# A spectral layer with other factors, and head and tail stages that share pools, in a forward-and-backward kernel on one Trainium2 core

## The chip, the cores and the metric

The kernel runs on one core of a Trainium2 chip (trn2). Times are device microseconds (us) of one execution, given as the median of several. A profile is one execution; its span is a little shorter than the time. A program on one core gave no slow run. TensorE, VectorE, ScalarE, GpSimd and SyncE are called PE, DVE, ACT, POOL and SP in the lines of the profile, and PEld is TensorE's weight load. An engine that starts DMAs holds a queue for them: SPq is the one of SyncE.

## The reference

One residual block, its output, and the gradients of all its inputs for a given output gradient. Everything is bfloat16 outside; S = 2048 positions, D = 576 channels, F = 4608 hidden channels.

```python
mod = (silu(c) @ w_mod).reshape(1, 6, 1, -1)            # sa, ca, ga, sb, cb, gb
h  = layernorm(x) * (1 + ca) + sa
x1 = x + ga * irfft2(rfft2(h) * (w_r + 1j * w_i))       # spectral layer over (S, D)
h2 = layernorm(x1) * (1 + cb) + sb
out = x1 + gb * (((h2 @ w_gate) * (h2 @ w_up)) @ w_down)
# returned: out, and d/d(x, w_r, w_i, w_gate, w_up, w_down, c, w_mod) of sum(out * grad_out)
```

## The kernel before

Three parts run one after another. The **head** computes the modulation, the first LayerNorm, the spectral layer forward, and the "gradient groups": the output gradient times the transposed `w_down`, stored to memory (`ghhT_d`) for later. The **main loop** has 18 iterations over the hidden channels: gate and up projections, their gradients and the three weight gradients. The change leaves its code alone. The **tail** computes the second LayerNorm's backward, the down-projection, the spectral layer backward, the first LayerNorm's backward, and the gradients of the modulation.

The spectral layer is a 2-D transform as matrix products. Before the change it went channel transform, 128-point transform, then, after a transpose on TensorE of 73 blocks, a 16-point transform whose output is scattered by strided evictions (an eviction, `evac` in the code, copies a result of TensorE out of PSUM, the memory that matmuls write to):

```python
def chainF(hT, T, ring, sm, fps, name):
    Vp = ring.tile([128, NG, 128], BF, name=name + "Vp", tag="r")     # NG = 73
    for t in range(NT):                                               # NT = 16
        for cc in range(2):
            for m in range(5):
                nc.tensor.matmul(zp[:, :FP], lhsT=hT[:, t, m, :], rhs=T["RD"][:, m, cc, :], ...)
            evac(zt[:, cc, :], zp[:, :FP])
        # ... [cut: 128-point transform into vp, strided eviction into Vp] ...
    dma_T(VT, Vp, fps)                     # transposes on TensorE, through PSUM
    for g0 in range(0, NG, 4):
        # ... [cut: 16-point transform, two strided evictions for each group of 4] ...
```

The gradient groups transpose `w_down` on TensorE.

```python
for j in range(FB4):
    for m in range(4):
        nc.tensor.transpose(ptw[:, m, :], wdn[:, j, m * 128:(m + 1) * 128], ident[:])
    # ... [cut: fifth block, evictions to wdT and wdL] ...
for j in range(0, FB4, 2):
    for sp in range(2):
        for k in range(2):
            for i in range(2):             # 64 rows: wdL, block 4
                nc.tensor.matmul(pts[k][i][:], lhsT=wdL[r, j // 2, :], rhs=goT[r, tss[k], 4, :], start=True, stop=False)
        for k in range(2):
            for i in range(2):
                for m in range(4):         # 128 rows
                    nc.tensor.matmul(pts[k][i][:], lhsT=wdT[:, m, ...], rhs=goT[:, tss[k], m, :], start=False, stop=(m == 3))
```

Each stage has its own pools, so a stage starts when the one before has given its memory back; tables are loaded as fp32 and cast; sums over rows go through GpSimd accumulators and a round trip through memory (`dm_d`).

## Time and profile before

| | before |
|---|---|
| time, median of 4 | 2083.85 us (2070.23 to 2090.29) |
| span of the profile | 2068.4 us |
| head, to the main loop's first 128-row matmul | 479 us |
| main loop, to its last matmul | 1007 us |
| tail | 582 us |

The boundaries in the table are starts and ends of single matmuls in the trace.

These are lines of the page of the kernel before. The first gives, for each engine, its busy time, share of the span and number of instructions. The others cut the span in 40 slices; a digit is the busy share of a slice in tenths, and PEclk is the granted clock of TensorE in tenths.

```profile
PE 1617.6 (78%) x11711; PEld 1058.5 (51%) x11711; DVE 1027.7 (50%) x2082; ACT 533.0 (26%) x1059; POOL 324.8 (16%) x329
...
PE   2086988399999999999999999999757982626321
...
DVE  1567776035443334444444444333486333388974
...
PEclk8587999699999999999999999999868995867555
```

The middle, slices 9 to 28, is a plain stretch of 9: TensorE is the bound there. On both sides TensorE falls to between 0 and 8 tenths in most slices, and its clock in many of them. The average of 78% hides that the two ends have another limit than the middle.

The table of stretches of the kernel before says where. Its columns are: stretch, its length, busy time (and instructions) of each engine, granted clock, DMA share, GB/s.

```profile
core 0: us, PE busy (x) PEld busy (x) DVE busy (x) ACT busy (x) POOL busy (x), PEclk, DMA share, GB/s
0.00:103.00 103.00, 14.80 (x71) 5.93 (x71) 39.23 (x90) 18.75 (x26) 20.35 (x25) 0.65 0.80 246
...
362.00:380.00 18.00, 0.00 (x0) 0.00 (x0) 0.07 (x1) 0.00 (x0) 0.00 (x0) 0.52 1.13 223
...
478.00:1486.00 1008.00, 1004.09 (x7776) 708.07 (x7776) 422.54 (x1008) 257.63 (x522) 93.19 (x134) 1.00 0.68 129
...
1887.00:2011.00 124.00, 43.48 (x182) 16.25 (x180) 106.68 (x123) 34.31 (x62) 86.52 (x49) 0.55 0.24 74
2011.00:2068.00 57.00, 6.66 (x16) 3.78 (x16) 21.57 (x16) 17.25 (x9) 0.00 (x0) 0.56 0.41 156
```

TensorE does 14.8 us of work in the first 103 us. From 362 to 380 no engine works at all. In the main loop it is busy 1004 of 1008 us. In the last 181 us it is busy 50 us, with the clock at half.

What holds everything at 362 is one instruction on SyncE's queue. Its line in the queue's timeline of the kernel before gives start, length, engine, source line and operands:

```profile
352.24 24.25 SPq L466 DMA_TRANSPOSE h2T<-h2p  x1
```

The stores of the gradients stand behind it on that queue (the next is issued at 376.6 us), and TensorE waits 20.0 us for the buffers that they hold.

And this is one group of DVE in the first LayerNorm's backward, of the kernel before: count, busy time in us, mean ns of one.

```profile
L737 DVE SCALAR_TENSOR_TENSOR t<-gn,n1b 128x576 bf16<-128x576 bf16 x16 | 22.9, 1430 | 0.6
```

### The profile page before, as it was taken

The page shows a single profiled execution, that of the slowest core. Times are in us where ns is not written, and L with a number is a line of the kernel's source. Part 1 is how long each engine was busy: PE and PEld are TensorE (multiplying, and loading weights), DVE is VectorE, ACT ScalarE, POOL GpSimd, SP SyncE. Part 2 cuts the span into 40 slices and gives each one's busy share as a digit, 9 for nine tenths or more (in the row PEclk, how much of TensorE's full clock was granted, in tenths as well). Part 3 has the DMA queues.
Part 4 walks back from the last instruction along what each step waited for, and adds up shares of the span by engine and source line. Part 5 has one row for each costly group of instructions (what it writes and reads, how often), then busy time and mean ns, then how long its engine had stood idle before and what let it go on. Part 6 is the DMA issues. An engine that isn't in the chain of part 4 may idle for free. (4 is left out here: it accounts for less than half of the span.)

```text
span 2068.4 us, 29648 instructions
## 1 busy us (share of the span) xinstructions
PE 1617.6 (78%) x11711; PEld 1058.5 (51%) x11711; DVE 1027.7 (50%) x2082; ACT 533.0 (26%) x1059; POOL 324.8 (16%) x329
## 2 busy tenths in 40 slices
PE   2086988399999999999999999999757982626321
PEld 0054533145666677777666666666635762423100
DVE  1567776035443334444444444333486333388974
ACT  1254533022222222222222222222110001234133
POOL 1200001001111001011111111100102335224740
PEclk8587999699999999999999999999868995867555
DMA  7834365537766666666677776675576633071223
GB/s 274 218 121 170 134 240 131 134 114 158 136 108 134 125 130 125 130 136 136 143 132 136 140 123 138 120 129 109 147 268 256 237 122 133 31 284 45 84 99 126
DMA packets 387660, 302.78 MB, mean 146 GB/s; under 512 B 305697, under 2 KB 352929, under 8 KB 382785
## 3 DMA queue, kind: packets, MB, share of 16 engines
q1 hardware_dynamic: 363808, 203.55, 39.8%
q0 software_dynamic: 23712, 97.34, 17.2%
q8 instruction: 91, 1.49, 0.3%
q14 instruction: 49, 0.39, 0.1%
HBM read 138.63 MB, written 89.71 MB: 110 GB/s over the span
## 5 line engine op out<-in xcount | busy, mean ns | idle before, releaser
L536 DVE TENSOR_TENSOR guT<-ghh,gT 128x512 bf16<-128x512 bf16 x144 | 61.2, 425 | 480.3 <-DMA out_dram<-wl 384.0
L553 PE MATMUL abp<-wT,guT 128*128 128x288 bf16 x1152 | 283.0, 286 | 0.0
L552 PE MATMUL abp<-wT,ggT 128*128 128x288 bf16 x1152 | 283.0, 286 | 0.0
L530 PE MATMUL abp<-h2T,wgu 128*128 128x512 bf16 x1152 | 261.1, 380 | 0.0
L558 DVE TENSOR_TENSOR acc<-acc,abp 128x288 f32<-128x288 f32 x544 | 240.7, 453 | 20.5 <-PE abp L553 5.3
L574 PEld LDWEIGHTS <-h2p 128*128 128x128 bf16 x2304 | 225.3, 98 | 26.7
L530 PEld LDWEIGHTS <-wgu 128*128 128x128 bf16 x1152 | 106.8, 98 | 149.5 <-issue 30.5
L542 POOL DMA_DIRECT2D hhT_d<-hhT x36 | 33.2, 923 | 911.4 <-DVE hhT L534 773.6
L648 PE MATMUL u3p<-wdr,hl 128*128 128x288 bf16 x1152 | 150.8, 294 | 23.0 <-DMA hl<-hhT_d 12.7
L426 PE MATMUL u4p<-goT,wdT 128*128 128x512 bf16 x576 | 161.6, 410 | 0.0
L566 PE MATMUL gwp<-gon,hh_sf 128*128 128x288 bf16 x1152 | 144.8, 286 | 3.0 <-DMA hh_sf<-hhT 3.0
L648 PEld LDWEIGHTS <-hl 128*128 128x128 bf16 x1152 | 115.4, 100 | 56.1 <-DMA hl<-hhT_d 13.2
L567 ACT CAST so<-gwp 128x288 bf16<-128x288 f32 x72 | 28.7, 398 | 394.3 <-PE gwp L566 394.3
L566 PEld LDWEIGHTS <-hh_sf 128*128 128x128 bf16 x1152 | 112.3, 98 | 32.5 <-DMA hh_sf<-hhT 4.3
L574 PE MATMUL gwp<-gg_sf,h2p 128*128 128x256 bf16 x1152 | 128.7, 273 | 0.0
L574 PE MATMUL gwp<-gu_sf,h2p 128*128 128x256 bf16 x1152 | 128.7, 273 | 0.0
L553 PEld LDWEIGHTS <-guT 128*128 128x128 bf16 x1152 | 112.6, 98 | 30.3
L552 PEld LDWEIGHTS <-ggT 128*128 128x128 bf16 x1152 | 112.7, 98 | 30.0
L311 PE MATMUL yp<-T_IR,ut 128*128 128x288 bf16 (+1 forms) x384 | 75.8, 334 | 55.9 <-ACT gh L731 55.9
L532 ACT CAST gT<-abp 128x512 bf16<-128x512 f32 x144 | 84.3, 585 | 85.4 <-PE abp L530 85.4
L575 ACT CAST wo<-gwp 128x256 bf16<-128x256 f32 x144 | 53.6, 372 | 197.5 <-PE gwp L574 196.1
L137 DVE CAST ghh_st<-u4p 128x512 bf16<-128x512 f32 x72 | 49.1, 688 | 110.8 <-PE u4p L426 59.9
(380 smaller groups left out, 2113.0 us busy)
## 6 DMA issues: line engine op xcount, KB each, us to landing
ghhT_d<-ghh_st SPq DMA_DIRECT2D x36, 512.0 KB, 3.2
ghh<-ghhT_d POOLq DMA_DIRECT2D x36, 512.0 KB, 9.5
hhT_d<-hhT POOLq DMA_DIRECT2D x36, 512.0 KB, 6.8
hl<-hhT_d SPq DMA_DIRECT2D x8, 2304.0 KB, 9.7
out_dram<-wo SPq DMA_DIRECT2D x36, 256.0 KB, 2.3
gxc<-gx_d SPq DMA_DIRECT2D x8, 1152.0 KB, 8.8
wm<-in_w_mod_dram SPq DMA_DIRECT2D x2, 3456.0 KB, 14.2
wdn<-in_B_w_down_dram SPq DMA_DIRECT2D x9, 576.0 KB, 6.7
```

What stands on the lines that cost most here:

```text
L311: nc.tensor.matmul(yp[:, 0:288], lhsT=ut[0:Kf, fc, cc * 128:(cc + 1) * 128], rhs=T["IR"][0:Kf, fc, cc, h * 288:(h + 1) * 288], start=(k == ...
L426: nc.tensor.matmul(pts[k][i][:], lhsT=wdT[:, m, (j + i) * 128:(j + i + 1) * 128], rhs=goT[:, tss[k], m, :], start=False, stop=(m == 3))
L530: nc.tensor.matmul(pts[k][i][:], lhsT=wgu[:, 4 * i + m, cs], rhs=h2T[:, ts_, m, :], start=False, stop=(m == 3))
L532: nc.scalar.copy(dst[:], pts[k][i][:])
L536: nc.vector.tensor_tensor(out=guT[:, ts_, :], in0=ghh[:, ts_, :], in1=gu[0][:], op=MUL)
L552: nc.tensor.matmul(pu[:, 0:288], lhsT=ggTs[j][:, t, :], rhs=wT[:, 0, j, hs_], start=(j == 0), stop=False)
L553: nc.tensor.matmul(pu[:, 0:288], lhsT=guTs[j][:, t, :], rhs=wT[:, 1, j, hs_], start=False, stop=(j == G - 1))
L558: nc.vector.tensor_tensor(out=dst, in0=dst, in1=pu[:, 0:288], op=ADD)
L566: nc.tensor.matmul(pw[:, 0:288], lhsT=hh_sf[:, j, t, :], rhs=gon[:, t, h * 288:(h + 1) * 288], start=(t == 0), stop=(t == NT - 1))
L574: nc.tensor.matmul(pw[:], lhsT=h2p[:, t, m * 128:(m + 1) * 128], rhs=sf[:, :, t, :], start=(t == 0), stop=(t == NT - 1))
L575: nc.scalar.copy(wo[:, m, :], pw[:].rearrange("q j f -> q (j f)"))
L648: nc.tensor.matmul(p2[h][:, 0:288], lhsT=hl[:, fb, ti * 128:(ti + 1) * 128], rhs=wdr[:, fb, h * 288:(h + 1) * 288], start=(fb == 0), stop= ...
```

## The change

It leaves the main loop alone and rewrites head and tail. The spectral layer does the 16-point step first (on rows that need no transpose), folds the channels into even and odd halves, and treats frequencies k and 16-k as a pair, so that each of 8 pairs is a short chain of matmul, eviction, matmul. Tables and intermediates are bfloat16. The transposed `w_down` comes by transposing DMA. GpSimd does no arithmetic; column sums are matmuls with a matrix of ones. And head and tail each have one set of pools for all their stages, so that the gradient groups (head) and the down-projection (tail) can fill TensorE while the chain of small operations runs elsewhere. Outside the main loop the order of each engine's instructions is fixed when the kernel is compiled; an engine then runs them in that order. The diff is 1454 lines; this is its core.

```diff
-def chainF(hT, T, ring, sm, fps, name): ...          # and to_group, chainI, make_hT, dma_T
+def fold(wk, h, t0, hT, T, fps, eng):                  # even/odd halves, then the 16-point step
+    nc.vector.tensor_tensor(out=eo[:, :, 0:256], in0=h[:, :, 0:256], in1=h[:, :, 576:320:-1], op=ADD)
+    # ... [cut: three more] ...
+    nc.tensor.matmul(ps[:, m, :, j, :], lhsT=eo[:, j, m * 128:(m + 1) * 128], rhs=T["BD"][:], start=True, stop=True)
+def pair_fwd(i, wk, gt, T, hT, fps, ev):               # one frequency pair forward
+    for kk, kap in enumerate((k2a, k2b)):
+        pz = fps.tile([128, 2, 512], FP32, name="pz", tag="fa")      # two PSUM slots in all
+        # ... [cut: 6 matmuls] ...
+        evac(zt[:, kk, :, :], pz[:, :, 0:FQ], ev[kk])
+    for kk in range(2):
+        px = fps.tile([128, 2, 512], FP32, name="px", tag="fa")
+        # ... [cut: 4 to 8 matmuls] ...
+        evac(X[:, kk, :, :], px[:, :, 0:FQ], ev[2 + kk])
+    return X
@@ gradient groups
-                nc.tensor.transpose(ptw[:, m, :], wdn[:, j, m * 128:(m + 1) * 128], ident[:])
+                nc.sync.dma_start_transpose(out=wdT[:, 0:4, :], in_=B_w_down[rows, 0:512])
+                nc.sync.dma_start_transpose(out=wdT[:, 4:5, :], in_=B_w_down[rows, 448:576])
+                for k in range(2):
+                    for b in range(2):
+                        for m in range(5):
+                            r = slice(0, 128) if m < 4 else slice(64, 128)
+                            nc.tensor.matmul(pg[:, b, :], lhsT=wdT[r, m, :], rhs=goT[r, ts_, m, :], start=(m == 0), stop=(m == 4))
@@ end of the head: the activations of the main loop, transposed in two pieces
-            nc.sync.dma_start_transpose(out=h2T[:]..., in_=h2p[:]...)
+                if t0 % 8 == 6:
+                    t8 = slice(t0 - 6, t0 + 2)
+                    nc.sync.dma_start_transpose(out=h2T[:, t8, :, :]..., in_=h2p[:, t8, :]...)
+                grad_group(NFB - 8 + t0 // 2, True)
@@ tail
+    for i in range(8):
+        Gy = pair_fwd(i, wk, gt, T, hT, fps, "aaaa")
+        Y = cmul(wk, Gy, load_wp(wk, i), True)
+        pair_inv(i, Y, gbt, ut, fps, "va")
+        # ... [cut: gradients of w_r and w_i] ...
+    # ... [cut: inverse transform and first LayerNorm's backward] ...
+    hl = slot(0, [128, NFB, 256], "hl")                  # down-projection, in the same pools
```

## The prediction

> **What bounds the kernel now.** The profiled span is 2068 us: head to 479, main loop to 1486, tail to the end (starts of single instructions). The table of stretches shows TensorE busy 892 of 895 us (535 to 1430) at clock 1.00: the main loop is bound by TensorE, and the change leaves its code alone. In head and tail no engine is the bound. TensorE is mostly idle for 95 us (fp32 tables are loaded and cast; `c` lands after 15 us behind a 3.4 MB load) and for 18 us at 362 (the transposing DMA of `h2p` holds the SP queue 24 us and the `ghh_st` stores wait). In the tail, stages run one after another: second-LayerNorm backward, down-projection (129 us, DVE busy 51), spectral backward at clock 0.5 to 0.8, first-LayerNorm backward (124 us, DVE busy 107; L737 takes 1430 ns beside GpSimd, the like L610 817), then 57 us of `dm_d` round trip and modulation gradients.
>
> **What the change does.** (1) Spectral transforms are refactored (16-point step first, even/odd folding, conjugate pairs); TensorE transposes and many strided evictions go. Counted matmul columns: head 552k against 563k, tail 553k against 561k. [...] (512-column matmuls start 216 ns apart). Estimated floor: 230 us each. (2) Transposed `w_down` comes by DMA. (3) bf16 tables, intermediates and modulation vectors. [...] 512 bf16 elements 425 ns, 576 fp32 750 ns. (4) GpSimd arithmetic and `dm_d`/`modb_d` round trips go; column sums move to TensorE. (5) Stages share pools, so gradient groups (head) and down-projection (tail) can fill TensorE while the chain runs on DVE and ACT.
>
> **Costs (estimates from traced durations).** Head: first gradient matmul near 30 us instead of 105; 218 us of TensorE work at 88% density; DVE 145, ACT 170 us beside it; last transposes: 300 us (before 479). Main loop: 1005 (1007). Tail: DVE 67 second LayerNorm, 63 pairs, 50 first LayerNorm, 44 modulation gradients, 18 down-projection: 242 us, of which 20 can start before the last weight gradients end. DVE and TensorE both near 230 us; with dependences 275 (582). All saving is on the critical path: the three parts are serial.
>
> **Prediction.** 300 + 1005 + 275, plus 10 for dispatch and last stores: **1590 us**, 8 in 10 between **1525 and 1680**. Faster by over 2%: 0.98; within: 0.01; slower: 0.01.
>
> **What would show each step.** First main-loop matmul at 275 to 330 us, then 1005 us unchanged. Head: TensorE at 8 to 9 tenths from 35 us. Tail 245 to 320 us: DVE 8 to 9 tenths, down-projection matmuls scattered between fold and pair matmuls, clock near 1.0. bf16 tensor_tensor of 1152 elements near 760 ns; GpSimd nearly idle.
>
> **What would make it wrong.** The scheduled order may put the down-projection last (tail +100 us). The single `hl` and output PSUM buffers could stall it. Two PSUM slots per chain could make pairs latency-bound (over 12 us each). [...] 72 small transposing DMAs may hold the SP queue and starve the gradient groups. Memory placement or DMA may slow the main loop.

The floor of 230 us for each end stands as an estimate: at the 216 ns for 512 columns that the trace of the kernel before shows, counts of 552k and 553k columns give 233 us. The 760 ns expected for 1152 bfloat16 elements lie on the line through two points of the same trace, 425 ns for a product of 512 elements and 2.57 us for one of 4624.

## More of the kernel before

A contraction of 576 is four blocks of 128 and one of 64. Note the order in which it is written: four 64-row matmuls first, then sixteen 128-row ones. The compiled order is another: the trace has 175 direct changes between its 64-row and its 128-row gradient matmuls, with only 144 of the former.

## The result, and the profile after

| | before | after |
|---|---|---|
| median, all runs of this pair | 2079.12 us (2070.23 to 2093.53, 16 runs) | 1717.72 us (1698.22 to 1723.57, 11 runs) |
| span of the profile | 2068.4 us | 1715.9 us |
| ratio | | 0.823, 95% interval 0.820 to 0.826 |

A ratio is the mean time of one kernel's runs over that of the other's of the same rounds, so it is not quite the ratio of the medians. The kernel takes 18% less time. It is 128 us slower than the predicted 1590 us, and 38 us above the top of the range.

The same lines of the page, for the kernel after:

```profile
PE 1560.4 (91%) x11196; PEld 1018.3 (59%) x11196; DVE 764.3 (45%) x1743; ACT 513.7 (30%) x881; POOL 202.8 (12%) x365
...
PE   3899999458999999999999999999999959998983
...
DVE  4733005332542355234533454235423767678831
...
PEclk9899999779999999999999999999999979999997
```

TensorE now stands at 8 and 9 almost everywhere. What is left are four notches: the first slice, slices 8 and 9 (300 to 386 us, the end of the head), slice 33 (1373 to 1416, the start of the tail), and the end.

The table of stretches of the kernel after, columns as before:

```profile
core 0: us, PE busy (x) PEld busy (x) DVE busy (x) ACT busy (x) POOL busy (x), PEclk, DMA share, GB/s
0.00:48.00 48.00, 17.75 (x71) 7.50 (x72) 20.66 (x61) 7.93 (x13) 7.82 (x19) 0.91 1.09 272
...
338.00:371.00 33.00, 8.06 (x29) 2.64 (x28) 9.46 (x22) 7.55 (x12) 8.42 (x14) 0.64 0.88 168
371.00:1385.00 1014.00, 1002.75 (x7753) 707.34 (x7752) 439.99 (x1054) 258.95 (x523) 99.84 (x148) 1.00 0.69 136
1385.00:1414.00 29.00, 13.20 (x117) 6.84 (x113) 16.97 (x38) 8.55 (x13) 8.82 (x20) 0.65 0.98 349
1414.00:1550.00 136.00, 129.70 (x1023) 94.36 (x1021) 98.85 (x169) 44.57 (x69) 24.03 (x54) 1.00 0.63 187
...
1690.00:1716.00 26.00, 2.43 (x8) 1.06 (x6) 6.08 (x15) 4.29 (x6) 1.62 (x3) 0.53 0.15 45
```

The first 48 us and the 29 us at 1385 have a DMA share near 1 (1.09 and 0.98): DMA engines, not TensorE, are full there. In the last 26 us every engine is idle for most of the time.

What TensorE waited for around the head's end, in the view of waits of the kernel after from 290 to 375 us (who waited, for what, us in total, times, longest):

```profile
PE ghp L377 <- DMA wdTh<-in_B_w_down_dram: 19.5, 1, 19.5
PE abp L480 <- DMA wgu<-in_B_w_gate_dram: 13.6, 1, 13.6
PE abp L480 <- DMA wgu<-in_B_w_up_dram: 9.8, 1, 9.8
```

Why the first of these came late is seen on SyncE's queue, of the kernel after:

```profile
295.47 10.85 SPq L418 DMA_TRANSPOSE h2T<-h2p  x1
306.49 1.84 SPq L368 DMA_TRANSPOSE wdTh<-in_B_w_down_dram  x1
308.39 1.22 SPq L369 DMA_TRANSPOSE wdTh<-in_B_w_down_dram  x1
309.78 6.84 SPq L368 DMA_TRANSPOSE wdTh<-in_B_w_down_dram  x1
```

The 24.25 us transpose of the kernel before is now two of about 11 us. The first still stands in front of the small transposes of `w_down`, and TensorE stands still for 19.5 us, which is the gap at 300 to 320 us.

And the line that answers to L737 of before:

```profile
L671 DVE SCALAR_TENSOR_TENSOR t<-gn,n1b 128x576 bf16<-128x576 bf16 x16 | 12.1, 754 | 0.3
```

The same operation on the same shapes takes 754 ns in the mean where it took 1430. But the mean misleads: in the kernel before, ten of the 16 took 757 or 758 ns, with GpSimd adding beside each of them (as far as the trace's rough times for GpSimd tell); six took 1825 to 4192. So arithmetic on GpSimd at the same time was not enough to slow it, and what set the six apart was not tested.

Set against the sum of the prediction, measured from the trace:

| part | predicted | after | difference |
|---|---|---|---|
| head, until the 17th 128-row matmul of the main loop | 300 | 371 | +71 |
| from there to the main loop's last matmul | 1005 | 1014 | +9 |
| from there to the end of the span | 275 | 331 | +56 |
| time less span (the prediction's 10 were for dispatch and last stores) | 10 | 2 | -8 |
| sum | 1590 | 1718 | +128 |

(The 17th is taken because after the first 16 the loop waits once more, 1.5 us, for its transposed activations; below, "the main loop flows" means this matmul. The first 128-row matmul, from which the 479 us of before are counted, starts at 363.6 us; by that boundary the head misses by 64 us and the loop by 17. In the kernel before, the 17th starts at 483.5 us.) The experiments have to explain 71 us of head and 56 us of tail.

### The profile page after: what moved, and what is told of

Same layout as the page of the kernel before. It is cut to its first block, busy times and chain, and to the rows that moved or that the text cites. A ratio compares the mean times of both kernels' runs of the same rounds, so it can differ in the third digit from the quotient of the medians.

```text
span 1715.9 us, 28314 instructions
## 1 busy us (share of the span) xinstructions
PE 1560.4 (91%) x11196; PEld 1018.3 (59%) x11196; DVE 764.3 (45%) x1743; ACT 513.7 (30%) x881; POOL 202.8 (12%) x365
## 4 chain that ended last, share of the span: by engine, by line
PE 82%; DMA 9%; DVE 3%; ACT 2%; issue 1%; SPq 1%; POOL 0%; DVEq 0%; ACTq 0%; POOLq 0%
PE abp L486 15%; PE gwp L530 14%; PE ghp L377 10%; PE abp L508 8%; PE abp L509 8%; PE gwp L522 7%; PE po L700 7%; PE pb L240 2%; PE abp L480 2%; PE gwp L537 2%; PE px L221 2%; DMA hh_sf<-hhT 2%; PE pv L269 1%; PE pz L206 1%; PE cs L556 1%; DMA h2T<-h2p 1%
## 5 line engine op out<-in xcount | busy, mean ns | idle before, releaser
L492 DVE TENSOR_TENSOR guT<-ghh,gT 128x512 bf16<-128x512 bf16 x144 | 61.2, 425 | 504.5 <-DMA out_dram<-wl 383.5
L700 PE MATMUL po<-wdr,hl 128*128 128x288 bf16 x1152 | 162.5, 291 | 21.8 <-DMA hl<-hhT_d 12.7
L377 PE MATMUL ghp<-goT,wdT 128*128 128x512 bf16 (+1 forms) x560 | 151.9, 386 | 3.4 <-DVE mods L325 2.3
L700 PEld LDWEIGHTS <-hl 128*128 128x128 bf16 x1152 | 111.4, 99 | 62.6 <-issue 21.4
L377 PEld LDWEIGHTS <-wdT 128*128 128x128 bf16 (+1 forms) x560 | 46.7, 97 | 97.4 <-issue 74.0
L488 ACT CAST uT<-abp 128x512 bf16<-128x512 f32 x144 | 84.3, 585 | 47.6 <-PE abp L486 45.8
```

The costliest lines, as they stand in the source:

```text
L377: nc.tensor.matmul(pg[:, b, :], lhsT=wdT[r, m, :], rhs=goT[r, ts_, m, :], start=(m == 0), stop=(m == 4))
L488: nc.scalar.copy(dst[:], pts[k][i][:])
L492: nc.vector.tensor_tensor(out=guT[:, ts_, :], in0=ghh[:, ts_, :], in1=gu[0][:], op=MUL)
L700: nc.tensor.matmul(po[:, h, 0:288], lhsT=hl[:, fb, j * 128:(j + 1) * 128], rhs=wdr[fb // 18][:, fb % 18, h * 288:(h + 1) * 288], start=(fb ...
```

## The experiments

Eighteen kernels ran, all with 3 or 5 timed rounds. The differences "from after" below are (ratio - 0.8232) x 2079 us. Each ratio has an interval of about +-6 us, so a difference from after of less than 8 us is not resolved by the times. Any edit also makes the compiler order other instructions differently, so an effect in one stage is read from that stage in the trace. That has a limit too: in runs that leave the tail's code alone (e1, e2, e3, e10, e18) the tail takes 322.1 to 330.9 us, and in runs that leave the head's alone (e4 to e9, e11) the main loop flows at 366.1 to 376.2 us. A single trace with a tail up to 9 us shorter, or a head up to 5 us shorter, than after proves nothing by that alone. "Tail" is from the main loop's last matmul to the end of the span: 330.7 us after.

| run | median us | ratio | from after |
|---|---|---|---|
| after | 1717.72 | 0.8232 | |
| e1_k128 | 1693.81 | 0.8148 | -17 |
| e2_pair64 | 1704.23 | 0.8204 | -6 |
| e3_h2t8 | 1696.49 | 0.8164 | -14 |
| e4_halfdown (wrong) | 1697.00 | 0.8174 | -12 |
| e5_tailload | 1707.81 | 0.8203 | -6 |
| e6_gcrow | 1692.58 | 0.8129 | -21 |
| e7_nogw (wrong) | 1706.91 | 0.8199 | -7 |
| e8_halfboth (wrong) | 1696.69 | 0.8153 | -16 |
| e9_pipe | 1706.82 | 0.8210 | -5 |
| e10_crow | 1719.19 | 0.8275 | +9 |
| e11_hllate | 1776.19 | 0.8561 | +68 |
| e12_best | 1666.93 | 0.8011 | -46 |
| e13_nocrow | 1666.11 | 0.8023 | -43 |
| e14_gradfirst | 1657.64 | 0.7977 | -53 |
| e15_pre | 1673.19 | 0.8042 | -39 |
| e16_all | 1656.81 | 0.7976 | -53 |
| e17_wmlate | 1674.70 | 0.8054 | -37 |
| e18_wmlate0 | 1739.02 | 0.8361 | +27 |

### Head: the order of 64-row and 128-row matmuls (e1_k128, e2_pair64)

From 172 to 253 us the kernel after runs gradient matmuls and nothing else. The starts of consecutive matmuls in the trace are 257 ns apart on average (314 matmuls in 80.9 us). That mean has two parts in the trace: 216 ns between two matmuls of 128 rows, and about 0.1 us more wherever the number of rows changes between 128 and 64. In the order of the change every fifth matmul has 64 rows, so there are two changes in five. From 48 to 338 us there are 283 changes, which cost 30.5 us together, 108 ns each.

e1_k128 fills the fifth block's other 64 rows with zeros in the weights, so that all matmuls have 128 rows. The result is the same.

```diff
+                nc.gpsimd.memset(wdT[0:64, 4, :], 0.0)
-                            r = slice(0, 128) if m < 4 else slice(64, 128)
-                            nc.tensor.matmul(pg[:, b, :], lhsT=wdT[r, m, :], rhs=goT[r, ts_, m, :], ...)
+                            nc.tensor.matmul(pg[:, b, :], lhsT=wdT[:, m, :], rhs=goT[:, ts_, m, :], ...)
```

> The changed kernel with the fifth matmul of every gradient accumulation run over all 128 rows (the unused 64 weight rows set to zero), so that no gradient matmul changes the number of rows. Theory A (a change between 128-row and 64-row matmuls costs about 107 ns each time, 283 times in the head, on the critical path): the solid gradient stretch falls from 257 to about 217 ns per matmul, the first main-loop matmul comes 20 to 30 us earlier, the whole kernel takes 1685 to 1700 us against 1718. Rival B (the row changes hide in the waits for DMA that follow): matmuls closer together, but the kernel stays at 1710 to 1720 us.

Measured: correct, 1693.81 us, ratio 0.8148. In the same stretch 350 gradient matmuls now take 75.9 us, 217 ns each, and there are no changes; the main loop flows at 354.0 us where it did at 371.1. So 17 of the 30 us came back; the waits around them stayed (the one for `w_down` is 19.4 us long here).

e2_pair64 keeps the 64-row matmuls and puts those of two neighbouring sums next to each other, which halves the changes.

```diff
-                        for m in range(5):
+                    for b, m in [(0, 0), (0, 1), (0, 2), (0, 3), (0, 4), (1, 4), (1, 0), (1, 1), (1, 2), (1, 3)]:
```

> The changed kernel with the two 64-row matmuls of each pair of accumulations put next to each other: as many 64-row matmuls as before, half the changes of row count. If the change of rows is what costs, the solid gradient stretch takes about 237 ns per matmul and about half of the saving of the 128-row variant appears (8 to 15 us). If the 64-row matmul itself is slow, 257 ns stay and the time stays near 1718 us.

Measured: correct, 1704.23 us, ratio 0.8204; not resolved by the times. The trace is clear: 160 changes in place of 283 cost 17.2 us in place of 30.5, and in the pure stretch the matmuls are 237 ns apart, half way between 257 and 217. (Its loop flows at 368.9 us, within the spread of the head.) The gradient matmuls in 67 us of solid work, in the view of stretches for their operand `wdT` alone (stretch, its length, PE and PEld busy with counts, for e1 also GpSimd, then clock, DMA share, GB/s), first in the kernel after, then in e2_pair64, then in e1_k128:

```profile
172.00:239.00 67.00, 66.98 (x260) 20.91 (x261) 1.00 0.40 126
```

```profile
175.00:242.00 67.00, 67.00 (x285) 23.02 (x284) 1.00 0.43 137
```

```profile
172.00:239.00 67.00, 67.00 (x312) 30.34 (x310) 2.57 (x13) 1.00 0.46 149
```

What follows: the cost belongs to the change of rows and not to the 64-row matmul. e1 alone could have meant that 64-row matmuls are slow; e2 has as many of them as before. The cost is not new with the change: the kernel before is written with groups of four, but its compiled order has 175 such changes. What the change did give up is another thing: in the kernel before, where two 64-row gradient matmuls on the two halves of the rows follow one another, they start 4 ns apart in the median (43 times, 25 of them within 27 ns; 11 times the next pair starts 222 to 224 ns later), so the two of a pair run at once; here each 64-row one takes its turn. The prediction took 88% density for everything in the head; this one term takes 30 us beside 225 us of column time.

### Head: long transposes on SyncE's queue (e3_h2t8)

```diff
-                if t0 % 8 == 6:
-                    t8 = slice(t0 - 6, t0 + 2)
+                if True:
+                    t8 = slice(t0, t0 + 2)
```

> The changed kernel with the transposing DMA of h2p issued in eight pieces of two tiles instead of two of eight. Theory A (one large transposing DMA holds the SP queue about 11 us, so the small transposes of w_down behind it come late and TensorE waits 19 us near 300 us, and the second one puts 21 us before the main loop): the wait near 300 us shrinks below 5 us, the main loop's first full matmuls start 15 to 25 us earlier, limited then by the gate and up weights at 12 us after the last LayerNorm; whole kernel 1693 to 1703 us. Rival B (it is the amount of transposed data, not the size of the piece): the waits only move, 1710 to 1720 us.

Measured: correct, 1696.49 us, ratio 0.8164. The wait for the transposed `w_down` fell from 19.5 us in one piece to 8.2 us in five, and the main loop flows at 348.0 us, 23 us sooner. The line of the waits of e3_h2t8, from 48 to 322 us:

```profile
PE ghp L377 <- DMA wdTh<-in_B_w_down_dram: 8.2, 5, 3.4
```

The whole gains 14 us by the ratio and 17 by the span; the main loop took 6 us longer in this trace. The pieces do not take less of the queue in sum: where three are issued back to back they hold it 22.0 us. But a small transpose that is needed now stands behind a short one, and the last piece is all that the main loop has to wait for.

### Tail: is it TensorE, VectorE, or the chain? (e4_halfdown, e8_halfboth, e7_nogw)

In the stretch 1414 to 1550 us TensorE is busy 130 of 136 us and DVE 99. If TensorE were the bound, the time would fall with its work. e4_halfdown leaves out every second half of the down-projection's sum (all loads kept), e8_halfboth leaves out those loads as well, and e7_nogw leaves out the DVE operations for the gradients of `w_r` and `w_i`.

```diff
-                for fb in range(NFB):
+                for fb in range(NFB // 2):
```

> Wrong result on purpose: the changed kernel with only half of the down-projection's matmuls (576 of 1152, about 70 us of TensorE at 122 ns), all loads kept. Theory A (the tail is bound by TensorE): the time from the end of the main loop to the end falls from 330 us by 50 to 70 us, whole kernel 1650 to 1668 us. Rival B (the tail is bound by the vector chain of LayerNorm, pairs and inverse, the down-projection fills holes): it falls by less than 30 us, 1690 to 1715 us.

> Wrong result on purpose: half of the down-projection's matmuls and also half of its loads (the variant before kept the loads and fell by only 17 us in the tail, ending with TensorE busy 24 of 57 us). Theory A (that variant was held by the loads of its single hl buffer, and the tail by TensorE work otherwise): the tail falls from 331 us by 40 to 65 us, kernel 1652 to 1676 us. Rival B (the vector chain is close behind TensorE): the tail falls by 15 to 30 us only, with the down-projection done before the last LayerNorm tiles.

```diff
-            nc.vector.tensor_tensor(out=pA[:], in0=Xl[:], in1=Gy[:], op=MUL)
-            # ... [cut: four more operations per pair] ...
+            gw = Gy
```

> Wrong result on purpose: the changed kernel without the five vector operations per pair that make the spectral weight gradients (about 5.4 us of VectorE per pair, 40 us in all, in fp32); the stores stay and take other data. Theory A (between 1414 and 1550 us TensorE is full, 120 us of column time in 136): the pairs keep 11 to 12 us each, the tail falls by less than 10 us, kernel 1708 to 1720 us. Rival B (the vector chain binds the pairs): the pairs fall to 9 us or less each, the tail by 20 to 40 us.

Measured: e4 1697.00 us, tail 314.0; e8 1696.69 us, tail 315.0; e7 1706.91 us, tail 322.2. Halving takes away 576 matmuls of 288 columns, about 70 us of column time (matmuls of 288 columns start 122 ns apart in the trace of the kernel after), and the tail gives back 16 to 17 us. Taking away 30 us of DVE work (DVE is busy 201 us in the tail after, 170 in e7) leaves a tail 8.5 us shorter, which is within the spread of tails that nobody edited; its pairs follow every 10.2 us where they did every 11.4, between the theory and the rival. The last matmul of the spectral layer's inverse, which ends the chain's transforms, starts at 1615 us after, at 1611 and 1617 in e4 and e8, and at 1604 in e7. So the chain does not care about the down-projection, and only a little about DVE. Neither engine alone is the bound of the tail.

The traces also show where halving did help. After the chain, the last five of the 16 output blocks of the down-projection run with hardly any other work, in the kernel after (360 matmuls) and in e8_halfboth (180). Their stretches, columns as in the tables above, after and then e8:

```profile
1637.80:1688.30 50.50, 47.50 (x368) 36.13 (x368) 7.24 (x12) 3.20 (x5) 5.09 (x10) 0.98 0.50 157
```

```profile
1640.50:1676.00 35.50, 27.94 (x189) 19.34 (x189) 7.41 (x12) 3.35 (x6) 5.40 (x10) 0.88 0.51 164
```

These 15 us are nearly all that e8 saved. In e8 TensorE is busy only 70 of 90 us while the pairs run (1460 to 1550 us), and still the same five blocks stand behind the chain. TensorE waits 5.1 and 3.6 us in front of them, for DVE, with small column sums that the order has first. So it is the compiled order that puts them there, and not a lack of room in front; whether another order would move them forward was not tried.

### Tail: the pairs as a chain (e9_pipe)

In the tail the pairs follow one another every 11.4 us (mean of the seven intervals between the first matmuls of consecutive pairs), while DVE has 7.9 us of work for each. In the order written, pair i+1's first matmuls come after pair i's last, which wait for pair i's multiplications on DVE; then DVE waits for pair i+1's four evictions on ACT. e9_pipe writes the forward half of pair i+1 ahead of the multiply and inverse half of pair i.

```diff
+        held = []
+        for step in range(9):
+            if step == 8:
+                i = 8
+            else:
+              i = step
+              # ... [cut: table loads, as before] ...
+              Gy = pair_fwd(i, wk, gt, T, hT, fps, "aaaa")
+              held.append((i, Gy, gbt))
+            if step == 0:
+                continue
+            i, Gy, gbt = held[step - 1]
             Y = cmul(wk, Gy, load_wp(wk, i), True)
             pair_inv(i, Y, gbt, ut, fps, "va")
```

> Edit: in the tail, the forward half of frequency pair i+1 is written ahead of the spectral multiply and inverse half of pair i, so the next pair's first matmuls do not queue behind the present pair's last ones. Same arithmetic, same buffers. Theory (the tail's pairs are bound by their own chain of matmul, eviction and next matmul, in the order written): the pair interval of 11.7 us in the kernel after falls to 9.5 us or less, the tail (331 us from the end of the main loop) by 10 to 25 us, the kernel to 1695 to 1710 us. Rival (TensorE is full there, with 120 of 136 us of column time because the down-projection fills the holes): the pairs go faster but the down-projection ends as late, tail and kernel move less than 5 us.

Measured: correct, 1706.82 us, ratio 0.8210. The group of DVE that begins a pair's multiplication, with the idle time of DVE just before it and what ended it, is in the kernel after, from 1448 to 1540 us:

```profile
L259 DVE TENSOR_TENSOR cA<-X,wn 128x1160 bf16<-128x1160 bf16 x8 | 6.1, 763 | 33.5 <-issue 17.8 <-ACT X L153 15.7
```

and in e9_pipe, from 1444 to 1520 us:

```profile
L259 DVE TENSOR_TENSOR cA<-X,wn 128x1160 bf16<-128x1160 bf16 x8 | 6.1, 757 | 1.1 <-issue 1.1
```

The pairs come every 8.4 us by the same mean; but the first interval is 3.1 us only because two forward halves now stand next to each other, and the other six average 9.3 us (11.8 after). The tail is 318.0 us, 12.7 less. The theory's numbers for interval and tail hold. The time of the whole moves by 5 us by the ratio and 11 by the medians, which the intervals do not resolve. What ends the gain is seen in the trace: the chain's last inverse matmul starts at 1592 us, 23 us sooner, but the last matmul of the down-projection is only 14 us sooner (1674 for 1688). With the chain shorter, TensorE's own work becomes the limit: from 1450 to 1520 us of e9_pipe it is busy 69.5 of 70 us, and DVE 61.2.

### Tail: what the overlap is worth (e11_hllate)

```diff
-        hl = slot(0, [128, NFB, 256], "hl")
+        hl = slot(1, [128, NFB, 256], "hl")
```

Slot 1 holds the operand of the forward pairs, so the down-projection has to wait until the last of them is done.

> Edit: the down-projection's operand shares the buffer that the spectral stage of the tail uses, so that the down-projection can start only when the last forward pair is done; this takes the overlap of the change's reordering away. Theory (the chain binds the tail, with the down-projection filling its holes): the chain shortens to what it takes alone, roughly 200 us, and the down-projection's 110 us of column time comes mostly after it; the first down-projection matmul starts near 1500 us, the kernel takes 30 to 90 us more than after, 1745 to 1805. Rival (the two hinder each other so much that overlap is worth nothing): within 10 us of after.

Measured: correct, 1776.19 us, ratio 0.8561: 68 us more than after by the ratio, in the expected range. The first down-projection matmul starts at 1539 us (1408 after). The table of stretches of e11_hllate:

```profile
1440.00:1540.00 100.00, 65.74 (x384) 43.70 (x382) 53.67 (x73) 25.93 (x41) 11.45 (x26) 0.81 0.41 115
...
1620.00:1772.00 152.00, 120.20 (x921) 89.85 (x920) 34.40 (x60) 22.27 (x33) 16.18 (x30) 0.92 0.49 148
```

One part of the expectation fell. The chain did not shorten to 200 us: its last inverse matmul starts at 1617 us, as late as after (1615), and the pairs come every 13.1 us, slower than with the down-projection beside them. The granted clock is 0.81 in that stretch, where after it was 1.00. So the chain takes about 230 us whether TensorE is filled or not, the overlap is worth some 56 us of tail, and filling TensorE costs the chain nothing that shows. (The lower clock may have lengthened e11's chain and hidden such a cost; no run separates the two. The first down-projection matmul was expected near 1500 us.)

### Tail: its two ends (e5_tailload, e6_gcrow)

At the tail's start the down-projection waits for its operand `hl`, whose load stands behind four loads of `w_down` on the queue. e5_tailload issues the two in turn.

```diff
-        for fb0 in range(0, NFB, 9):
-            nc.sync.dma_start(wdr[...], B_w_down[...])
         hl = slot(0, [128, NFB, 256], "hl")
         for tp_i in range(NT // 2):
             for fb0 in range(0, NFB, 9):
+                if tp_i == 0:
+                    nc.sync.dma_start(wdr[...], B_w_down[...])
                 nc.sync.dma_start(hl[:, fb0:fb0 + 9, :], hhT_d[tp_i, :, fb0:fb0 + 9, :])
```

> The changed kernel with the loads of w_down and of the first hl issued alternately, in four steps, instead of all four of w_down first. Theory A (the down-projection starts 23 us after the main loop because its first hl piece stands behind 5.3 MB of w_down in the SP queue): the first down-projection matmul comes 10 to 16 us after the main loop's end, the kernel takes 1705 to 1713 us. Rival B (the DMA engines are full there whatever the order, at 366 GB/s): start within 4 us of the old distance, 1714 to 1722 us.

Measured: correct, 1707.81 us, ratio 0.8203, not resolved. The first down-projection matmul starts 9 us after the main loop's end, not 23, and the tail is 325.0 us, 6 less, which is within the spread of tails that nobody edited. A wait of 14 us was taken away, and at most 6 came back.

At the other end stands one line of the DMA view of the kernel after, from 1699 us on: what was stored, from which queue, size, and us from issue to landing.

```profile
out_dram<-gcf SPq DMA_DIRECT2D x1, 1.0 KB, 14.3
```

This is the gradient of `c`, one KB, written as 512 separate elements of two bytes (the last 64 go likewise). The trace shows 638 packets under 512 bytes in those 17 us, and 14.3 us to land; in e6_gcrow, whose edit follows, it is 26 such packets in the last 4 us. e6_gcrow turns the columns into rows with one small matmul and stores rows.

```diff
-            nc.sync.dma_start(out_7[0, 0:512].rearrange("(m q) -> q m", q=128), gcf[:, 0:4])
+        nc.tensor.matmul(pt[0:5, 0, 0:128], lhsT=gcf[:], rhs=ident[:], start=True, stop=True)
+        nc.vector.tensor_copy(gct[0:5, :], pt[0:5, 0, 0:128])
+        nc.sync.dma_start(out_7[0, 0:512].rearrange("(m q) -> m q", q=128), gct[0:4, :])
```

> The changed kernel with g_c turned into five rows by one small matmul and stored as rows of 256 bytes, instead of 576 separate elements of 2 bytes (landing after 14.2 us). If that scattered store is what the last 14 us wait for: the time from the last down-projection matmul to the end falls from 28 to about 17 us, kernel 1704 to 1710 us. If landing takes as long with rows (a fixed cost at the end): no change, 1714 to 1722 us.

Measured: correct, 1692.58 us, ratio 0.8129. From the last down-projection matmul to the end it is 14.5 us, where it was 27.7. That is 13 us of the 21 that the ratio shows; the rest was not traced to a cause, and is no more than the spread of unedited tails. The kernel before has the same scattered store (13.7 us to land), so this is no cost of the change: the prediction had 10 us for dispatch and last stores together, and this store alone takes 14.3.

### Head: why the first gradient matmul starts at 48 us (e10_crow, e13_nocrow, e14_gradfirst)

The prediction said 30 us. `c` is loaded in the same scattered way and lands after 12.3 us; the modulation, the scaling of the output gradient and its transposes (`goT`) follow from it. e10_crow loads rows.

```diff
-                nc.sync.dma_start(c_bf[:, 0:4], c_in[0, 0:512].rearrange("(m q) -> q m", q=128))
+            nc.sync.dma_start(c_bf[0:4, :], c_in[0, 0:512].rearrange("(m q) -> m q", q=128))
+            nc.tensor.matmul(pc[:, 0, 0:5], lhsT=c_bf[0:5, :], rhs=ident[0:5, 0:5], start=True, stop=True)
```

> Edit: c is loaded as five rows and turned into columns by one small matmul, in place of 576 elements of two bytes each. Theory (the head's start is late because of that scattered load): c is there 8 to 10 us sooner, the first modulation matmuls start near 8 us in place of 16, the first gradient matmul near 42 us in place of 48, kernel 4 to 9 us faster. Rival (the transfers that fill the DMA engines up to 40 us set the first gradient): the modulation starts sooner, the first gradient stays within 2 us of 48, and the kernel is the same.

Measured: correct, 1719.19 us, ratio 0.8275: no gain. The theory fell; the rival is right that nothing was gained and wrong about the first gradient. The modulation did start 7 us sooner (9.3 us for 16.2), and the transposes were issued at 25.0 us for 28.9. But the first gradient matmul starts at 71.7 us. TensorE's timeline of e10_crow shows why:

```profile
66.62 1.03 PE L194 MATMUL s1p<-T_BD,eo 128*128 128x128 bf16 x8 [2.32 <-DVE eo L186]
67.45 0.42 PE L198 MATMUL s1t<-T_BD,eo 128*128 128x128 bf16 x2
71.74 0.58 PE L381 MATMUL ghp<-goT,wdT 128*128 128x512 bf16 x1 [3.87 <-DVE mods L331]
```

The compiler put all folds ahead of the gradients, and TensorE idles between them, waiting for DVE, with gradient work at hand: `goT` had landed by 47.0 us (its second transpose was issued at 33.8 us and landed 13.2 us later). The main loop flows at 386.4 us, 15 us later than after.

e12_best puts together the parts of e1, e3, e5, e6, e9 and e10, with no other lines:

> Edit: the parts that helped, together: zero-padded fifth contraction block (no 64-row matmuls), head's last transposes in eight pieces, alternate loads at the tail's start, the last gradient stored as rows, c loaded as rows, and the tail's pairs pipelined. Theory (they act on different stages of one serial program, so gains add): 20 to 24 from the padding, about 20 from the eight pieces, 13 from the stored rows, 6 from the loads, 4 to 9 from c, up to 15 from the pairs, less what overlaps: 1630 to 1665 us, and the head's main loop starts before 330 us. Rival (each edit's gain was largely the same slack found in another place): no better than 1675.

Measured: correct, 1666.93 us, ratio 0.8011: 2 us above the expected range, between the two theories. Its first gradient was as late as e10's, at 73.3 us. Was e10's part to blame? e13_nocrow takes it out again:

> Edit: the combined version (e12_best, 1666.9 us) with c loaded as scattered elements again. Theory (loading c as rows did not help because the fixed order of TensorE's instructions, which is made when the kernel is compiled, then put the first gradient matmul behind all the folds, at 73 us): without that edit the first gradient is back near 48 us, the main loop starts 8 to 15 us sooner than in e12_best's 341.5 us, kernel 1645 to 1662. Rival (the first gradient's time does not matter because the loads set the head): main loop start and kernel within 4 us of e12_best.

Measured: correct, 1666.11 us, ratio 0.8023, first gradient at 73.6 us. The theory fell: without the edit the order is as bad, so the order is not a consequence of loading `c` as rows; other edits give it too. e14_gradfirst therefore sets the order: in e12_best, the first three gradient groups are written ahead of the folds.

```diff
+            for fb in range(3):
+                grad_group(fb)
             hT = slot(0, [128, 5, 16, 128], "hT")
             for t0 in range(0, NT, 2):
                 # ... [folds] ...
-            for fb in range(NFB - 8):
+            for fb in range(3, NFB - 8):
```

> Edit: e12_best with the first three gradient groups written ahead of the folds of the spectral layer, so that they have the earlier place in TensorE's order. Theory (with c early and the gradients in front, the first gradient starts when the transposes of the scaled output gradient land): first gradient at 38 to 44 us, main loop start before 330 us, kernel 1640 to 1655. Rival (the transposing DMAs, over 30 us of one queue between 8 and 45 us, and full DMA engines set the start): first gradient at 44 us or later, and the fold work is pushed back by as much, kernel within 5 us of e12_best.

Measured: correct, 1657.64 us, ratio 0.7977, 9 us less than e12_best by the medians and 7 by the ratio, which the times alone do not resolve. The main loop flows at 330.1 us, where it did at 347.5 in e12_best. The first gradient starts at 43.9 us, at the edge of both theories, and not at about 34, which an issue at 19.8 us and the 13.8 us to landing of the kernel after would allow. What it waits for, from the view of waits of e14_gradfirst from 0 to 80 us:

```profile
PE ghp L362 <- DMA goT<-gon: 19.9, 1, 19.9
```

So after the order the transposes of `goT` are next. In this kernel they are issued at 19.8 us, at once when their operand is ready, and hold the queue 26.3 us.

### Head: contention, or the transposes' own length? (e17_wmlate, e18_wmlate0)

e17_wmlate is e14_gradfirst with the loads of the three modulation blocks that are needed last held back until the folds are done; e18_wmlate0 does the same to the kernel after.

```diff
+                if after is not None:
+                    nc.vector.tensor_copy(wm[:, :, 0:1], after)     # the load has to wait for this
                 eng.dma_start(wm[:, 0:4, :], w_mod[0:512, ...])
-            mod_block(MGA, nc.scalar)
+            mod_block(MGA, nc.scalar, hT[:, :, 0, 127:128])         # and likewise MSB, MCB
```

> Edit: e14_gradfirst, with the loads of the three modulation blocks that are needed only after the spectral layer (2 MB) held back until the last fold is done, by a one-column copy into their buffers. Theory (the transposes of the scaled gradient, which were issued at 19.8 us in e14_gradfirst and held their queue for 26.3 us in place of 17, are slowed by those loads on full DMA engines): they take 20 us or less, the first gradient starts at 35 to 39 us in place of 43.9, kernel 1645 to 1655, that is 3 to 9 us less than e14_gradfirst. Rival (the transposes are slow by themselves or wait for something else): first gradient at 42 us or later, the same time.

> Edit: the kernel after, with nothing but those three loads held back. Theory: the transposes of the scaled gradient, issued at 28.9 us, take a few us less than 17.1; first gradient at 42 to 46 us in place of 48, kernel 1710 to 1716. Rival: first gradient within 1 us of 48 or later by the compiler's order, kernel unchanged.

Measured: e17 1674.70 us, e18 1739.02 us; both correct, both slower. As edits they are misses: in e18 the first gradient fell to 90.4 us, because its place in TensorE's order came behind the late modulation matmuls; in e17 it came at 52.6 us. But the length of the two transposes is telling. These lines give their shortest, median and longest time on the queue in ns, and their first and last start in us; each moves 40 blocks of 128 x 128 elements. In e18_wmlate0:

```profile
L339 SPq DMA_TRANSPOSE goT<-gon x2: 6093/6570/7047, 27.3 to 34.5; - x2
```

In the kernel after:

```profile
L337 SPq DMA_TRANSPOSE goT<-gon x2: 7797/8508/9219, 28.9 to 36.8; - x2
```

In e14_gradfirst:

```profile
L341 SPq DMA_TRANSPOSE goT<-gon x2: 10422/13094/15767, 19.8 to 35.7; - x2
```

In e17_wmlate:

```profile
L343 SPq DMA_TRANSPOSE goT<-gon x2: 13193/17343/21493, 19.9 to 41.5; - x2
```

In these four runs the same transposes take 6.1 to 21.5 us. In e18 the modulation loads are held back, and GpSimd's queue starts no load in the 24.5 us before 40.9 us; in e14 and e17 the transposes are issued just when GpSimd's queue has started four loads of `x` and four of the spectral tables (18.8 to 23 us), and there they are longer, with or without the modulation loads. So they have no fixed length, and the theory that the modulation loads stretch them holds on the kernel after (13.2 us on the queue in place of 17.1; in the eight kernels that start as after does, the two take 16.8 to 23.1 us) and falls on e14. That the other loads do it is likely from the timing, but no run took those loads alone away. Two runs of the next section added one, though: e15_pre is e12_best with a load of 0.6 MB (the main loop's first weights) issued right after the transposes start, and with fewer work buffers. In e12_best:

```profile
L341 SPq DMA_TRANSPOSE goT<-gon x2: 9325/11858/14392, 25.0 to 34.5; - x2
```

In e15_pre:

```profile
L343 SPq DMA_TRANSPOSE goT<-gon x2: 16113/20954/25795, 25.3 to 51.2; - x2
```

That is 42.0 us on the queue in place of 23.8, and e16_all against e14_gradfirst has 31.3 in place of 26.3. This points to contention with whatever is in flight; which load it is in e14, and how much each one costs, stays open. Putting the transposes on another engine's queue was not tried.

### The main loop's first loads (e15_pre, e16_all)

TensorE waits 13.6 + 9.8 us for the first gate and up weights. Their load is issued at 348.0 us, behind the head's last store on GpSimd's queue. e15_pre gives them a buffer of their own and loads them during the head (and pays with 13 in place of 15 work buffers in the head and 2 in place of 3 staging buffers); e16_all is that and e14_gradfirst.

```diff
+            nc.gpsimd.dma_start(wgu0[:, 4 * wi_:4 * wi_ + 4, :], wsrc[0:512, 0:256]...)   # in the head
-        wgu = load_w(0)
+        wgu = wgu0
```

> Edit: e12_best with the main loop's first gate and up weights loaded 50 us before the head ends, into a buffer of their own (paid for with 13 in place of 15 work buffers in the head and 2 in place of 3 staging buffers in the main loop). Theory (TensorE's idle time of 13.2 + 1.8 us at the main loop's start is the wait for that load, which stands on GpSimd's queue behind the head's last store): that wait goes, main loop starts within 6 us of the last gradient, kernel 10 to 16 us less than e12_best. Rival (the other inputs of the first iteration, the last piece of the transposed activations and the gradients read back from memory, come no sooner): the wait moves to one of them, under 5 us gained.

> Edit: e12_best with both, the gradients in front and the early weight load. Theory (they act on two different waits, the head's start and the main loop's start): the gains of e14_gradfirst and e15_pre add within 5 us; kernel 1628 to 1645. Rival (the 13 work buffers hold the head back, or one wait hides the other): no better than the better of the two.

Measured: e15 1673.19 us, ratio 0.8042; e16 1656.81 us, ratio 0.7976; both correct, neither better than the version it was built on. The view of waits of e15_pre from 300 to 400 us has no line for the weights any more, and this one instead:

```profile
PE abp L489 <- DMA h2T<-h2p: 24.4, 1, 24.4
```

The first 128-row matmul of the loop starts 6.6 us after the last gradient, about as the theory said (6), and then the loop waits 24.4 us for the last pieces of its transposed activations. The rival holds: the wait moved to another input. The load itself did not stand where it was meant to: the compiler moved it forward to 25.9 us, among the transfers that fill the head's start, and the first gradient came at 82.1 us, 9 us later than in e12_best, after the long transposes shown above. The main loop's first iteration takes 85 us in e15 and e16, for 65 in e12_best and 55.8 in the steady state.

## Why the prediction was right or wrong, point by point

Two steps of the prediction failed. In the head (71 us) it was the sum of "first gradient matmul near 30 us", "218 us of TensorE work at 88% density" (248 us) and 22 us to the main loop: these measured 48, 290 and 33 us. In the tail (56 us) it was the overlap: "DVE and TensorE both near 230 us; with dependences 275" allowed 33 us over the 242 us of DVE work for a chain through both engines that took 230 us by itself, with 101 us behind it. What follows takes them one by one.

**Right: the direction, and which parts are serial.** All of the gain came from head and tail. The main loop's steady iteration takes 55.7 to 55.8 us in both kernels; the whole of it came out 9 us longer than predicted, and 11.5 longer than before between the same two matmuls, in the first iteration and in waits of 8.4 us for the transposed hidden activations (3.0 before).

**Right: the floor of TensorE.** The prediction had 230 us of column time for each end. Estimated for the matmuls that the trace of the kernel after has, from the gaps between starts that it shows (in the median 216 ns at 512 columns, 123 at 288, 109 at 256, 56 at 128), it is 233 us in the head and 238 in the tail.

**Right: the times of the bfloat16 operations, GpSimd's exit and the clock.** A bfloat16 tensor_tensor of 1152 elements takes 740 to 760 ns (predicted 760), and an addition of 512 elements with one operand read in reverse takes 420 to 421 ns in the median, no more than the 425 of one in order. L737's mean of 1430 ns became 754, though its median was 758 before. GpSimd's 203 us of busy time are now issues of DMAs (200 us) and memsets. The mean granted clock is 0.963 for 0.877.

**Right in the main: the order was not so bad that the whole down-projection came last.** e11_hllate shows what that would have cost: 56 us of tail. But the risk that the prediction named came true in part, with five of the 16 blocks behind the chain.

**Wrong: "first gradient matmul near 30 us instead of 105".** It was 48. That is 18 us of the head's 71. Experiments showed two limits, one behind the other: the place of the gradients in TensorE's fixed order (e10, e13: 72 to 74 us; e14: 44 us), and the transposes of the scaled gradient on full DMA engines (a DMA share of 1.16 from 20 to 40 us in the kernel after and in e14), 6 to 26 us each for the same work (e14 to e18). The scattered load of `c`, which I took for the culprit, was not shown to be it: removing it alone gained nothing. But removing it also changed the order, and no run has the good order with the scattered load. What exactly stretches the transposes stays open.

**Wrong: "218 us of TensorE work at 88% density".** From 48 to 338 us the density was 225 of 290 us, 78%. 88% left room for 30 us of all losses. The changes between 64 and 128 rows took those 30 us alone (e1, e2; without them the loop flows 17 us sooner), and 27 us of waits came on top, 19.5 of them for `w_down` behind one long transpose (e3). The prediction named that risk ("may hold the SP queue and starve the gradient groups") and put no time on it; and it named the 72 small transposes, where the two long ones did it. It did not see the changes of rows at all, though they stand in the trace of the kernel before too.

**Wrong, by 11 us: the end of the head.** From the last gradient to the flowing main loop it is 33 us (22 were left for it): weights, then the last transposed piece. e3 and e15 show that there are two waits in series; taking either alone leaves the other.

**Wrong: "with dependences 275" for the tail.** The sums were fair: DVE is busy 201 us in the tail (the four stretches from 1385 us, one of them not shown above) for the predicted 222, TensorE has its 238 us of columns. But 275 assumed that one of them would be the bound and the dependences would add a little. The runs show a chain of 230 us that neither halving TensorE's work (e4, e8) nor cutting DVE's (e7) shortens much, and that takes as long with the down-projection out of its way (e11). Behind it come about 73 us until the last matmul of the down-projection: 23 us with the end of the first LayerNorm's backward and of its modulation gradients, and 50 us of the five blocks that the compiled order left for the end. Then come 28 us of serial end, 14 of them one scattered store (e6). In the terms of the prediction: pairs were put at 63 us of DVE work and took 91 (8 of 11.4 us); "latency-bound (over 12 us each)" stood among the risks and came nearly true, for the order in which the pairs were written: e9 keeps the slots and gets 9.3 us in the steady state. What the slots cost was not tested.

**The terms together.** e12_best has the 64-row padding, the pieces, the alternate loads, the stored and loaded rows and the pipelined pairs; with the gradients in front (e14_gradfirst) it takes 1657.64 us, 60 less than after by the medians and 53 by the ratio, and is inside the predicted range. Head and tail are then 330 and 302 us. Of the 128 us that were missing, these runs account for the cause of 53 to 60 by removing it; the rest is seen in the trace (in e14_gradfirst the first 44 us, 15 us of waits for the main loop's first weights, a tail still 27 us over the prediction), but no version here is free of it.

## What to carry to other kernels

Price every named risk, and let the density of an engine be a sum of named losses: here one loss that nobody had named, alternating 64-row and 128-row matmuls, was as large as the whole allowance. When two engines each have as much work as the time allowed, ask for the length of the chain through both, and test it by taking work away: here halving one engine's work gave back a quarter of what it took away, the chain was the bound, and writing the next item's first half ahead of this item's second half made it 23 us shorter. Then look in the trace at what the compiled order leaves behind the chain. Removing the wait that is named first often uncovers another behind it (order, then transposes; weights, then transposed activations), so look at all inputs of the waiting instruction before you pay for one.
